# A hand-ordered weave of attention and MLP with three PSUM banks in turn and v scaled on Pool, on one Trainium2 core

## The chip, the cores and the metric

The kernel runs on one core of one Trainium2 chip. The metric is the device time of one execution in microseconds (us), median over the runs of a kernel. The profile covers the span from the first to the last instruction, which is 1 to 2.4 us shorter than the device time.

Names used below: PE is the tensor engine (PEld its weight loads), DVE the vector engine, ACT the scalar engine, POOL or Pool the GpSimd engine, SP the queue that issues most DMA. A *pair* is two heads of one batch element; there are 32 pairs, four per batch element.

## The reference

```python
# q, k, v: (8, 8, 576, 64)   omega: (128, 64)   w_in: (512, 2048)   w_out: (2048, 512)
def phi(x):                                     # x already scaled by 1/sqrt(sqrt(64))
    h = x @ omega.T - (x * x).sum(-1, keepdims=True) / 2
    return exp(h - h.max(-1, keepdims=True)) / sqrt(128)
kv  = einsum('bhsm,bhsd->bhmd', phi(k), v);  z = phi(k).sum(2)
att = einsum('bhsm,bhmd->bhsd', phi(q), kv) / (einsum('bhsm,bhm->bhs', phi(q), z) + 1e-6)
x   = att.transpose(0, 2, 1, 3).reshape(4608, 512)
h   = x @ w_in
out = (h * sigmoid(1.702 * h)) @ w_out          # float32
```

Both kernels use bf16 products. They drop what cancels in the ratio (the row factor of phi(q)), and divide v by the row maximum of exp(k-projection), which is the same as subtracting the maximum first.

## The kernel before

One head at a time is loaded, projected and normalised. A scheduler with priorities interleaves this with the MLP of finished tokens. Loads take 64 floats (256 bytes) per run, because a partition gets one token's head row.

```python
ps_tq = ...(bufs=2)   # transposes and q projection
ps_k  = ...(bufs=1)   # k projection, two banks
ps_nk = ...(bufs=1)
ps_h  = ...(bufs=2)   # first MLP product: two banks
ps_o  = ...(bufs=1)   # second MLP product: one bank
# ... (cut)
nc.gpsimd.dma_start(qkh[:, :, 0:64],
    qrows[row0 : row0 + SPAD, :].rearrange("(t p) d -> p t d", p=128))   # 256-byte runs, cast to bf16
# ... (cut)
def moe_block(tok0, ntok):                       # 512 tokens
    for f in range(NFC):                         # 16 quanta of the first product
        ph = ps_h.tile(...)
        for c in range(CM): nc.tensor.matmul(ph[:, 0:ntok], lhsT=win[...], rhs=xt[c][...], ...)
        nc.scalar.activation(out=th, in_=ph, func=AF.Tanh, scale=0.851)
        nc.vector.scalar_tensor_tensor(out=gT[:, f, 0:ntok], in0=th, scalar=1.0, in1=ph, op0=ALU.add, op1=ALU.mult)
    for r0 in range(0, ntok, 128):
        po = ps_o.tile(...)
        for f in range(NFC): nc.tensor.matmul(po[0:m, :], lhsT=gT[:, f, r0 : r0 + m], rhs=wout[:, f, :], ...)
        nc.scalar.activation(out=osb, in_=po, func=AF.Copy, scale=0.5)
        nc.sync.dma_start(out[...], osb)
```

The softmax here doesn't subtract the row's maximum and nothing guards it: scores larger than these inputs give would overflow.

Of the kernel before, what the change touches and what calls it, by code (L numbers as in the profile page):

```python
# [10 lines left out]
AF = mybir.ActivationFunctionType  # L12
ALU = mybir.AluOpType
# [3 lines left out]


@with_exitstack
def kernel(  # L20
# [10 lines left out]
    nc = tc.nc  # L31

    B, H, S, D = q.shape
    M_F = omega.shape[0]
    DM = H * D
    DFF = moe_w_in.shape[1]
    NT = B * S
    SCALE = 1.0 / math.sqrt(math.sqrt(D))

    assert M_F == 128 and D == 64 and DM == 512 and S == 576  # L40
    NCH = 5
    SPAD = NCH * 128
    CM = DM // 128
    NFC = DFF // 128
    TOK_BLK = 512
    last_b0 = (B - 1) * S
    blocks = []
    t0 = 0
    while t0 + TOK_BLK <= last_b0:
        blocks.append((t0, TOK_BLK))  # L50
        t0 += TOK_BLK
    if t0 < last_b0:
        blocks.append((t0, last_b0 - t0))
        t0 = last_b0
    while t0 < NT:
        n = min(TOK_BLK, NT - t0)
        blocks.append((t0, n))
        t0 += n

    const = ctx.enter_context(tc.tile_pool(name="const", bufs=1))  # L60
    xtp = ctx.enter_context(tc.tile_pool(name="xt", bufs=1))
    stage = ctx.enter_context(tc.tile_pool(name="stage", bufs=3))
    work = ctx.enter_context(tc.tile_pool(name="work", bufs=3))
    small = ctx.enter_context(tc.tile_pool(name="small", bufs=4))
    xbp = ctx.enter_context(tc.tile_pool(name="xb", bufs=2))
    gtp = ctx.enter_context(tc.tile_pool(name="gt", bufs=2))
    thp = ctx.enter_context(tc.tile_pool(name="th", bufs=3))
    osbp = ctx.enter_context(tc.tile_pool(name="osb", bufs=2))
    ps_tq = ctx.enter_context(tc.tile_pool(name="ps_tq", bufs=2, space=bass.MemoryType.PSUM))
    ps_k = ctx.enter_context(tc.tile_pool(name="ps_k", bufs=1, space=bass.MemoryType.PSUM))  # L70
    ps_nk = ctx.enter_context(tc.tile_pool(name="ps_nk", bufs=1, space=bass.MemoryType.PSUM))
    ps_h = ctx.enter_context(tc.tile_pool(name="ps_h", bufs=2, space=bass.MemoryType.PSUM))
    ps_o = ctx.enter_context(tc.tile_pool(name="ps_o", bufs=1, space=bass.MemoryType.PSUM))

    prio_stack = ExitStack()
    prio_stack.enter_context(tc.high_priority(offset=3_000_000))
    ident = const.tile([128, 128], BF16, name="ident")
    make_identity(nc, ident[:])

    om_f = const.tile([128, D], F32, name="om_f")  # L80
    nc.sync.dma_start(om_f[:], omega[:, :])
    om_b = const.tile([128, D], BF16, name="om_b")
    nc.vector.tensor_copy(out=om_b[:], in_=om_f[:])
    omT2 = const.tile([128, M_F], BF16, name="omT2")
    omt_ps = ps_tq.tile([128, SPAD], BF16, name="omt_ps", tag="tq")
    nc.tensor.transpose(omt_ps[0:64, 0:128], om_b[:], ident[:])
    nc.vector.tensor_copy(out=omT2[0:64, :], in_=omt_ps[0:64, 0:128])
    nc.vector.tensor_copy(out=omT2[64:128, :], in_=omt_ps[0:64, 0:128])

    win = const.tile([128, CM, DFF], BF16, name="win")  # L90
    wout = const.tile([128, NFC, DM], BF16, name="wout")

    win_pieces = [(c, j) for c in range(CM) for j in range(4)]
    wout_pieces = list(range(NFC))

    def load_win_piece(c, j):
        nc.gpsimd.dma_start(
            win[:, c, j * 512 : (j + 1) * 512],
            moe_w_in[c * 128 : (c + 1) * 128, j * 512 : (j + 1) * 512],
        )  # L100

    woutst = ctx.enter_context(tc.tile_pool(name="woutst", bufs=4))
    wout_stage = {}

    def load_wout_piece(f):
        t = woutst.tile([128, 1, DM], F32, name="wout_p", tag="wout_p")
        nc.sync.dma_start(t[:, 0, :], moe_w_out[f * 128 : (f + 1) * 128, :])
        wout_stage[f] = t

    def cast_wout_piece(f):  # L110
        nc.vector.tensor_copy(out=wout[:, f : f + 1, :], in_=wout_stage[f][:])

    xt = [xtp.tile([128, NT], BF16, name=f"xt{c}", tag=f"xt{c}") for c in range(CM)]
    prio_stack.close()

    qrows = q.rearrange("b h s d -> (b h s) d")
    krows = k.rearrange("b h s d -> (b h s) d")

    def attention_head(b: int, h: int, xb):
        qkh = stage.tile([128, NCH, 128], BF16, name="qkh", tag="qkh")  # L120
        vst = stage.tile([128, NCH, 65], F32, name="vst", tag="vst")
        row0 = (b * H + h) * S
        if (b, h) != (B - 1, H - 1):
            nc.gpsimd.dma_start(  # L124
                qkh[:, :, 0:64],
                qrows[row0 : row0 + SPAD, :].rearrange("(t p) d -> p t d", p=128),
            )
            nc.gpsimd.dma_start(  # L128
                qkh[:, :, 64:128],
                krows[row0 : row0 + SPAD, :].rearrange("(t p) d -> p t d", p=128),  # L130
            )
        else:
            nc.gpsimd.dma_start(
                qkh[:, 0:4, 0:64], q[b, h, 0:512, :].rearrange("(t p) d -> p t d", p=128)
            )
            nc.gpsimd.dma_start(
                qkh[:, 0:4, 64:128], k[b, h, 0:512, :].rearrange("(t p) d -> p t d", p=128)
            )
            nc.gpsimd.memset(qkh[64:128, 4, :], 0.0)
            nc.gpsimd.dma_start(qkh[0:64, 4, 0:64], q[b, h, 512:576, :])  # L140
            nc.gpsimd.dma_start(qkh[0:64, 4, 64:128], k[b, h, 512:576, :])
        nc.gpsimd.memset(vst[64:128, 4, :], 0.0)
        nc.gpsimd.memset(vst[:, 0:4, 64:65], 1.0)
        nc.gpsimd.memset(vst[0:64, 4, 64:65], 1.0)
        nc.sync.dma_start(
            vst[:, 0:4, 0:64], v[b, h, 0:512, :].rearrange("(t p) d -> p t d", p=128)
        )
        nc.sync.dma_start(vst[0:64, 4, 0:64], v[b, h, 512:576, :])

        qkTp = ps_tq.tile([128, SPAD], BF16, name="qkTp", tag="tq")  # L150
        for t in range(NCH):
            nc.tensor.transpose(qkTp[:, t * 128 : (t + 1) * 128], qkh[:, t, :], ident[:])  # L152
        qkT = work.tile([128, SPAD], BF16, name="qkT", tag="qkT")
        nc.vector.tensor_copy(out=qkT[:], in_=qkTp[:])  # L154

        qeT = work.tile([128, SPAD], BF16, name="qeT", tag="qeT")
        for c0, cn in ((0, 512), (512, 128)):
            pq = ps_tq.tile([128, 512], F32, name="pq", tag="tq")
            nc.tensor.matmul(pq[:, 0:cn], lhsT=omT2[0:64, :], rhs=qkT[0:64, c0 : c0 + cn])  # L159
            nc.scalar.activation(  # L160
                out=qeT[:, c0 : c0 + cn], in_=pq[:, 0:cn], func=AF.Exp, scale=SCALE
            )

        pk = ps_k.tile([128, NCH, 128], F32, name="pk", tag="pk")
        for t in range(NCH):
            nc.tensor.matmul(  # L166
                pk[:, t, :],
                lhsT=qkT[64:128, t * 128 : (t + 1) * 128],
                rhs=omT2[64:128, :],
            )  # L170
        ke = work.tile([128, NCH, 128], BF16, name="ke", tag="ke")
        nc.scalar.activation(out=ke[:], in_=pk[:], func=AF.Exp, scale=SCALE)  # L172
        maxE = small.tile([128, NCH], F32, name="maxE", tag="maxE")
        nc.vector.reduce_max(out=maxE[:], in_=ke[:], axis=AX.X)  # L174
        emax = small.tile([128, NCH], F32, name="emax", tag="emax")
        nc.vector.reciprocal(out=emax[:], in_=maxE[:])
        vp = work.tile([128, NCH, 65], BF16, name="vp", tag="vp")
        nc.vector.tensor_tensor(  # L178
            out=vp[:],
            in0=vst[:],  # L180
            in1=emax[:].unsqueeze(2).to_broadcast([128, NCH, 65]),
            op=ALU.mult,
        )

        nk = ps_nk.tile([128, 512], F32, name="nk", tag="nk")
        kvp = nk[:, 447:512]
        for t in range(NCH):
            nc.tensor.matmul(  # L188
                kvp,
                lhsT=ke[:, t, :],  # L190
                rhs=vp[:, t, :],
                start=(t == 0),
                stop=(t == NCH - 1),
            )
        kvs = work.tile([128, 65], BF16, name="kvs", tag="kvs")
        nc.scalar.activation(out=kvs[:], in_=kvp, func=AF.Copy)

        nd = nk[:, 0:NCH * 65].rearrange("p (t c) -> p t c", t=NCH)
        for t in range(NCH):
            nc.tensor.matmul(  # L200
                nd[:, t, :],
                lhsT=qeT[:, t * 128 : (t + 1) * 128],
                rhs=kvs[:],
            )
# [119 lines left out]
```

## Time and profile before

| | before |
|---|---|
| device time, median of 2 | 433.06 us (432.79 to 433.33) |
| span of the profile | 431.9 us |
| first MLP matmul starts | 53.29 us |
| last PE instruction ends | about 428.0 us |
| DMA packets under 512 bytes | 124,032 of 132,778 |

From the page of the kernel before: the busy tenths of PE in 40 equal slices of the span (a 9 is 90% or more), and the start of the chain that ended last, as shares of the span by line.

```profile
PE   0066597889988899989999899989999999999895
...
PE po L260 18%; PE ph L237 12%; DVE gT L248 3%; ACT th L245 3%; ACT osb L268 1%; ACT qeT L160 1%; PE qkTp L152 1%; PE nk L200 1%; PE xps L222 0%; PE pq L159 0%; PE nk L188 0%; DVE vp L178 0%; ACT ke L172 0%; DVE xb L209 0%; PE pk L166 0%
```

PE does almost nothing in the first two slices and is near full later. In the chain, lines 248, 245 and 268 (gT on DVE, th and osb on ACT) hold about 7%, 31 us, in which some later matmul waited for them.

From the chain in order of time, kernel before, in the stretch where only MLP work is left. The columns are start in us, length in us, and what ran (xN counts instructions).

```profile
311.44 0.93 PE ph L237 x4
...
312.40 0.61 ACT th L245
...
313.03 0.70 DVE gT L248
...
313.77 1.04 PE ph L237 x4
```

Four matmuls (0.87 us at full pace), then tanh, then gT, and only then the next four into that bank: this is the round of one of the two ph banks. PE's own timeline of the same stretch shows what it did meanwhile (start, length, line, operation and shape; xN counts instructions):

```profile
312.20 0.38 PE L237 MATMUL ph<-xt_116,win 128*128 128x512 bf16 x1
...
313.07 0.59 PE L260 MATMUL po<-wout,gT 128*128 128x512 bf16 x2
313.77 0.38 PE L237 MATMUL ph<-xt_116,win 128*128 128x512 bf16 x1
```

A block of 512 tokens takes 29.1 us here, where 128 matmuls at their 0.2157 us spacing would take 27.6.

From PE's timeline of the kernel before, in the woven part (start, length, line, operation and shape; xN counts instructions). The operation `ph` is the MLP, `pq` and `pk` are the q and k projections, 64 rows each.

```profile
219.31 0.38 PE L237 MATMUL ph<-xt_119,win 128*128 128x512 bf16 x1
219.63 0.38 PE L159 MATMUL pq<-qkT,omT_106 64*128 64x512 bf16 x1
219.64 0.40 PE L166 MATMUL pk<-omT_106,qkT 64*128 64x128 bf16 x4
219.85 0.22 PE L159 MATMUL pq<-qkT,omT_106 64*128 64x128 bf16 x1
219.87 0.22 PE L166 MATMUL pk<-omT_106,qkT 64*128 64x128 bf16 x1
220.02 0.39 PE L260 MATMUL po<-wout,gT 128*128 128x512 bf16 x1
```

pq and pk start together: they sit in different row halves of the array.

### The profile page before, as it was taken

The page shows a single profiled execution, that of the slowest core. Times are in us where ns is not written, and L with a number is a line of the kernel's source. Part 1 is how long each engine was busy: PE and PEld are TensorE (multiplying, and loading weights), DVE is VectorE, ACT ScalarE, POOL GpSimd, SP SyncE. Part 2 cuts the span into 40 slices and gives each one's busy share as a digit, 9 for nine tenths or more (in the row PEclk, how much of TensorE's full clock was granted, in tenths as well). Part 3 has the DMA queues.
Part 4 walks back from the last instruction along what each step waited for, and adds up shares of the span by engine and source line. Part 5 has one row for each costly group of instructions (what it writes and reads, how often), then busy time and mean ns, then how long its engine had stood idle before and what let it go on. Part 6 is the DMA issues. An engine that isn't in the chain of part 4 may idle for free. (4 is left out here: it accounts for less than half of the span.)

```text
span 431.9 us, 8223 instructions
## 1 busy us (share of the span) xinstructions
PE 372.1 (86%) x2801; PEld 189.3 (44%) x2801; DVE 276.9 (64%) x787; ACT 208.5 (48%) x454; POOL 139.3 (32%) x345
## 2 busy tenths in 40 slices
PE   0066597889988899989999899989999999999895
PEld 0044344454555454445455445444434444444342
DVE  1378769897799878889789878872351441523501
ACT  1044166565576545666467546633452433434412
POOL 8378256256266157256356336000000000000000
PEclk9999999999999999999999999999999999999999
DMA  9999589579799479669879759101101001011011
GB/s 163 248 257 174 63 67 103 66 73 139 120 80 97 70 85 143 93 54 124 130 79 101 81 74 133 38 2 49 50 0 73 27 24 74 1 49 38 7 67 37
DMA packets 132778, 36.21 MB, mean 84 GB/s; under 512 B 124032, under 2 KB 126080, under 8 KB 132736
## 3 DMA queue, kind: packets, MB, share of 16 engines
q0 software_dynamic: 86176, 12.58, 41.5%
q1 hardware_dynamic: 46560, 23.11, 19.4%
q8 instruction: 22, 0.36, 0.4%
q14 instruction: 20, 0.16, 0.1%
HBM read 38.80 MB, written 9.44 MB: 112 GB/s over the span
## 5 line engine op out<-in xcount | busy, mean ns | idle before, releaser
L260 PE MATMUL po<-wout,gT 128*128 128x512 bf16 (+1 forms) x592 | 163.5, 380 | 3.3 <-ACT osb L268 1.8
L248 DVE SCALAR_TENSOR_TENSOR gT<-th,ph 128x512 bf16<-128x512 bf16 (+2 forms) x160 | 99.2, 625 | 93.5 <-ACT th L245 92.8
L245 ACT ACTIVATE th<-ph 128x512 bf16<-128x512 f32 (+2 forms) x160 | 88.4, 555 | 69.1 <-PE ph L237 57.5
L237 PEld LDWEIGHTS <-win 128*128 128x128 bf16 x640 | 56.2, 98 | 58.2 <-issue 13.3
L124 POOL DMA_DIRECT2D qkh<-in_q_dram x63 | 54.7, 868 | 82.0 <-PE qkTp L152 69.6
L260 PEld LDWEIGHTS <-gT 128*128 128x128 bf16 (+1 forms) x592 | 53.7, 98 | 55.2 <-DVE gT L248 5.8
L160 ACT ACTIVATE qeT<-pq 128x512 bf16<-128x512 f32 (+1 forms) x128 | 49.2, 435 | 56.8 <-PE pq L159 43.9
L237 PE MATMUL ph<-xt_116,win 128*128 128x512 bf16 (+2 forms) x160 | 57.2, 360 | 8.4 <-DVE gT L248 6.6
L174 DVE TENSOR_REDUCE maxE<-ke 128x5 f32<-128x640 bf16 x64 | 52.1, 814 | 8.3 <-ACT ke L172 8.1
L237 PE MATMUL ph<-xt_117,win 128*128 128x512 bf16 (+2 forms) x160 | 57.3, 361 | 0.0
L237 PE MATMUL ph<-xt_118,win 128*128 128x512 bf16 (+2 forms) x160 | 57.0, 359 | 0.0
L237 PE MATMUL ph<-xt_119,win 128*128 128x512 bf16 (+2 forms) x160 | 57.0, 359 | 0.0
L128 POOL DMA_DIRECT2D qkh<-in_k_dram x63 | 54.8, 871 | 1.8 <-DMA qkh<-in_k_dram 0.8
L268 ACT ACTIVATE osb<-po 128x512 f32<-128x512 f32 (+1 forms) x37 | 22.1, 598 | 67.6 <-PE po L260 67.6
L159 PE MATMUL pq<-qkT,omT_106 64*128 64x512 bf16 (+1 forms) x128 | 31.8, 320 | 17.5 <-DVE qkT L154 17.3
L172 ACT ACTIVATE ke<-pk 128x640 bf16<-128x640 f32 x64 | 45.6, 712 | 0.3
L152 PE MATMUL qkTp<-ident,qkh 128*128 128x128 bf16 x320 | 31.2, 230 | 12.3 <-DMA qkh<-in_k_dram 5.9
L154 DVE COPY qkT<-qkTp 128x640 bf16<-128x640 bf16 x64 | 30.9, 483 | 12.7 <-PE qkTp L152 11.3
L152 PEld LDWEIGHTS <-qkh 128*128 128x128 bf16 x320 | 24.3, 102 | 33.0 <-issue 28.4
L178 DVE TENSOR_TENSOR vp<-vst,emax 128x325 bf16<-128x325 f32 x64 | 30.6, 478 | 1.4 <-DVE rden L208 0.4
L209 DVE TENSOR_TENSOR xb<-nk,rden 128x320 bf16<-128x320 f32 x64 | 31.0, 484 | 0.3
L166 PE MATMUL pk<-omT_106,qkT 64*128 64x128 bf16 x320 | 31.1, 230 | 0.0
(38 smaller groups left out, 263.1 us busy)
## 6 DMA issues: line engine op xcount, KB each, us to landing
out_dram<-osb SPq DMA_DIRECT2D x35, 256.0 KB, 2.0
vst<-in_v_dram SPq DMA_DIRECT2D x64, 128.0 KB, 2.7
qkh<-in_q_dram POOLq DMA_DIRECT2D x63, 80.0 KB, 3.1
qkh<-in_k_dram POOLq DMA_DIRECT2D x63, 80.0 KB, 3.4
wout_p<-in_moe_w_out_dram SPq DMA_DIRECT2D x16, 256.0 KB, 6.1
win<-in_moe_w_in_dram POOLq DMA_DIRECT2D x16, 128.0 KB, 6.6
vst<-in_v_dram SPq DMA_DIRECT2D x64, 16.0 KB, 2.7
out_dram<-osb SPq DMA_DIRECT2D x2, 128.0 KB, 2.3
```

The costliest lines, as they stand in the source:

```text
L124: nc.gpsimd.dma_start(qkh[:, :, 0:64], qrows[row0 : row0 + SPAD, :].rearrange("(t p) d -> p t d", p=128),)
L128: nc.gpsimd.dma_start(qkh[:, :, 64:128], krows[row0 : row0 + SPAD, :].rearrange("(t p) d -> p t d", p=128),)
L152: nc.tensor.transpose(qkTp[:, t * 128 : (t + 1) * 128], qkh[:, t, :], ident[:])
L159: nc.tensor.matmul(pq[:, 0:cn], lhsT=omT2[0:64, :], rhs=qkT[0:64, c0 : c0 + cn])
L160: nc.scalar.activation(out=qeT[:, c0 : c0 + cn], in_=pq[:, 0:cn], func=AF.Exp, scale=SCALE)
L166: nc.tensor.matmul(pk[:, t, :], lhsT=qkT[64:128, t * 128 : (t + 1) * 128], rhs=omT2[64:128, :],)
L172: nc.scalar.activation(out=ke[:], in_=pk[:], func=AF.Exp, scale=SCALE)
L174: nc.vector.reduce_max(out=maxE[:], in_=ke[:], axis=AX.X)
L237: nc.tensor.matmul(ph[:, 0:ntok], lhsT=win[:, c, f * 128 : (f + 1) * 128], rhs=xt[c][:, tok0 : tok0 + ntok], start=(c == 0), stop=(c == CM ...
L245: nc.scalar.activation(out=th[:, 0:ntok], in_=ph[:, 0:ntok], func=AF.Tanh, scale=0.851)
L248: nc.vector.scalar_tensor_tensor(out=gT[:, f, 0:ntok], in0=th[:, 0:ntok], scalar=1.0, in1=ph[:, 0:ntok], op0=ALU.add, op1=ALU.mult,)
L260: nc.tensor.matmul(po[0:m, :], lhsT=gT[:, f, r0 : r0 + m], rhs=wout[:, f, :], start=(f == 0), stop=(f == NFC - 1),)
```

## The change

Its intent: q, k and v come in pairs of heads, with 9 tokens of 64 floats per partition, so 2304-byte runs; both heads of a pair use the two row halves of the array; batch 0 is ordered by hand; from then on the MLP is cut into 288 *quanta* of four 512-column matmuls, and every step of a pair has a fixed quantum. The three MLP banks are separate tiles used in turn by both products. In batch 0 v is scaled on Pool. The diff, cut to its core:

```diff
-    ps_h = ctx.enter_context(tc.tile_pool(name="ps_h", bufs=2, space=bass.MemoryType.PSUM))
-    ps_o = ctx.enter_context(tc.tile_pool(name="ps_o", bufs=1, space=bass.MemoryType.PSUM))
+        tr = psum.tile([128, 1024], BF16, name="tr")          # transposes, one bank
+        pqk = psum.tile([128, 2, 512], F32, name="pqk")       # projections
+        nd = psum.tile([128, 2, 512], F32, name="nd")         # kv, numerator, denominator, rest of K
+        mo = [psum2.tile([128, 512], F32, name=f"mo{i}") for i in range(3)]
+    def pairs_of(x):
+        return x.rearrange("b (c e) (p t) d -> (b c) (e p) (t d)", e=2, t=NS)
+        def load_v(i, eng=nc.sync):
+            eng.dma_start(t[:], vv[i])
+        def KV(i):                                            # head e in row half e
+            for s in range(NS):
+                for e in range(2):
+                    nc.tensor.matmul(nd[:, e, 0:65], lhsT=ke[64 * e : 64 * e + 64, s, :],
+                                     rhs=t[64 * e : 64 * e + 64, s, :], ...)
+        def X(i, tr=tr):
+            for g in range(NG):
+                n = 128 if g < 4 else 64
+                nc.tensor.transpose(tr[:, g * 128 : g * 128 + n], xb[0:n, g, :], ident[0:n, 0:n])
... (cut: batch 0 by hand)
+        A(2)                   # transposes and their evictions
+        C(1)                   # q projection
+        Dv(1)                  # hm, m, em, and v scaled on Pool
+        load_win(2)
+        Bk(2)                  # K projection and its exps
+        ND(0)
+        xm(0)
+        expQ(1, pq2[:])
+        KV(1)
+        kvs(1)
+        A(3)
... (cut: the weave; s is the first quantum of pair i)
+                at(s, lambda: T1(i), lambda: evT1(i))
+                at(s + 1, lambda: T2(i), lambda: evT2(i))
+                at(s + 2, lambda: K(i))
+                at(s + 2, lambda: KV(i - 1), lambda: kvs(i - 1))
+                at(s + 2, lambda: expM(i), lambda: expK(i))
+                at(s + 3, lambda: ND(i - 1))
+                at(s + 3, lambda: mx0(i))                     # hm
+                at(s + 4, lambda: xm(i - 1))                  # xb
+                at(s + 5, lambda: Q(i, pqk), lambda: mx1(i), lambda: expQ(i, pqk[:]))
+                at(s + 6, lambda: X(i - 1), lambda: evX(i - 1))
+                at(s + 6, lambda: vp(i))
+                dst = mo[nb % 3][:]
```

Pairs 4 to 8 start every 5 quanta, from quantum 5, the later ones every 8.

## The prediction

> **What bounds the kernel now.** Three stretches, read from PE's timeline. (1) Start: the first MLP matmul begins at 53.3 us; until then PE waits on loads and on batch 0's chain through PE, ACT and DVE. (2) Weave, 53 to about 288 us: PE is 89 to 94% busy in the windows table, partly small matmuls and modelled tails. (3) Pure MLP, 288 to 432 us: five blocks, 29.1 us each in the chain of waits. A 512-column matmul starts every 0.2157 us, so a block of 128 needs 27.6 us, all nine 248.4 us. The chain gives DVE gT 3.1%, ACT th 2.7%, ACT osb 1.4%: 31 us in which PE stands because the two ph banks and the one po bank aren't free.
>
> **What the change does, costed from the trace.**
> - Start. q, k, v arrive as pairs of heads in 2304-byte runs instead of 256-byte ones. From packet times (a 2 KB run cast on the POOL queue takes about 0.1 us on one of 16 engines) a pair needs about 2.6 us, batch 0 about 10 us; before, 256-byte runs (32 ns each) competed with wout, and the first qkT copy came at 19.5 us. Four pairs at about 3.7 us (ACT: two exps of 1024 at 0.95 us; evictions) plus about 10 us of chain: first MLP matmul at about 30 us (26 to 36). v scaled on Pool: 576 elements, 1.3 us, an estimate from the Trainium skill, "GPSIMD Engine Reference", section "Performance versus the Vector engine" (about 2.6 cycles per element for two inputs); the trace has no such Pool arithmetic. Gain about 23 us.
> - Three banks in turn. Matmuls 0.86, tanh 0.60, gT 0.70: about 2.25 us per round, over three banks 0.75, under PE's 0.86. MLP becomes PE bound, 27.6 us a block. Gain about 30 us, most of the chain's DVE and ACT share.
> - Attention on PE. Transposes space at 56 ns, 65-column matmuls at 32 ns; pq and pk already start together, on different row halves. With both heads' K, Q and kv products paired over row halves I estimate 2.2 to 2.3 us a pair against about 2.9 now. 28 woven pairs: gain about 17 us.
> - DVE per woven pair, from back-to-back spacing (duration less 0.08 us): 0.60 + 0.37 + 0.67 + 0.67 + 0.74 + 0.37 + two reciprocals 0.4 = 3.8 us. In eight first-product quanta with a pair: DVE 4.9 + 3.8 = 8.7 us, ACT about 7.3, PE 6.9 + 2.2 = 9.1. PE leads only narrowly, so I add about 11 us of stalls, including the first pairs (every five quanta), where transposes wait for evictions of the one tr tile and qk tiles 5 to 7 land behind wout.
>
> **Sum.** 30 + 248.4 + 28 x 2.25 (63) + 11 stalls + 3 tail = about 355 us.
>
> Predicted: 355 us, 338 to 374 in 8 of 10. Faster by over 2%: 0.97; within: 0.02; slower: 0.01.
>
> **What would show it.** First MLP matmul near 30 us; last two blocks 27.6 us each, PE starts 0.216 us apart, no gT or th in the chain; blocks with four pairs 37 to 39 us; DVE about 90% busy in first-product stretches; DMA packets under 512 B nearly gone; Pool vp near 1.3 us.
>
> **What would make it wrong.** Pool vp at 2 us or more, setting the start's cadence, since DMA issue shares its queue; pair loads no faster; PE idle long in the start and then at half rate (0.43 us spacing at 53 us before); a fixed order stalling PE on every DVE or ACT delay (up to 375 us); paired row halves not overlapping for the kv product (plus 0.3 us a pair, 8 us).

## The result, and the profile after

| | before | after |
|---|---|---|
| device time, median of 2 | 433.06 us | 377.36 us (377.04 to 377.68) |
| span of the profile | 431.9 us | 375.9 us |
| first MLP matmul starts | 53.29 us | 35.58 us |
| first MLP matmul to the last | 374.7 us | 335.6 us |
| an unwoven MLP block | 29.1 us | 27.7 us |
| DMA packets under 512 bytes | 124,032 | 2,960 |

The ratio is 0.8703 (95% interval 0.8653 to 0.8753): the mean time of one kernel's fast runs over that of the other's of the same rounds, so not quite the ratio of the medians quoted. The change is a clear gain, but 377.4 us lies above the predicted range of 338 to 374. Of the 56.0 us that the span lost, 17.7 came from the start and 39.1 from the time between the first and the last MLP matmul; the tail grew by 0.8.

What the 39.1 us are made of can be read from both traces, by adding up the times from the start of one MLP matmul to the start of the next:

| between MLP matmuls, us | before | after |
|---|---|---|
| their own spacing at full rate | 252.1 | 248.5 |
| beyond it, where attention work lies between | 106.5 | 81.5 |
| beyond it, where nothing lies between | 15.9 | 5.5 |

Attention on PE, with the waits inside it, gave back 25 us, where the prediction had put 17. The MLP's own standing gave back 10.4, of 15.9 that there were to give, where the prediction had put 30 (waits for MLP banks that fall into the second row can't be told apart). The first row fell by 3.6 us because the kernel before cuts the tokens into eight blocks of 512, one of 448 and one of 64, and so needs 592 matmuls of the second product, where nine blocks need 576.

From the page of the changed kernel, the two lines that answer to those of before:

```profile
PE   6557998899999999999999999999999999999995
...
PE mo L301 30%; PE mo L281 17%; DVE gT L295 10%; ACT th L291 4%; DVE xb L255 4%; DVE m L201 3%; DVE qkT L118 2%; DVE vp L214 2%; PE nd L243 2%; PE nd L225 2%; ACT ke L172 2%; PE tr L266 2%; DVE xt L272 2%; DMA qk<-in_q_dram 2%; PE tr L108 2
```

The share of gT and th in the chain is still 14%. This is no contradiction, as the next views show: it all lies in the woven part. The chain at the end of the changed kernel:

```profile
315.86 13.92 PE mo L281 x64
329.77 13.81 PE mo L301 x64
343.59 13.81 PE mo L281 x64
357.40 13.83 PE mo L301 x64
```

In the last two blocks PE is the whole chain: 64 matmuls in 13.8 us, 0.216 us each. That is what three banks were meant to do. In the woven part the chain runs differently; here is one stretch of the first product (the 16 first quanta of a block):

```profile
126.96 0.64 ACT th L291
...
127.62 0.69 DVE gT L295
...
128.47 0.82 DVE xb L255
129.30 0.60 DVE gT L295
129.89 0.68 DVE m L201
...
130.72 0.63 DVE gT L295
131.35 0.37 DVE xt L272
131.72 0.67 DVE vp L214
132.38 1.20 DVE gT L295 x2
133.58 0.61 DVE qkT L118
...
134.23 0.22 PE tr L143
```

The lines left out here are small (reciprocals, and `issue` pieces of at most 0.09 us). From 127.6 to 134.2 us DVE works without a pause worth the name, and PE (`tr` at 134.23) waits for its end. Two windows of eight quanta each with one pair, the first in the first product and the second in the second product. The columns are length, busy time (and count) of PE, PEld, DVE, ACT and POOL, then granted clock (of PE, as the profile records it; 1.00 is full speed), DMA share and GB/s:

```profile
122.98:133.45 10.47, 10.06 (x89) 4.93 (x87) 8.92 (x17) 7.61 (x16) 1.05 (x2) 1.00 0.50 124
144.31:153.78 9.47, 9.47 (x87) 4.81 (x86) 4.11 (x8) 4.10 (x9) 1.05 (x2) 1.00 0.49 97
```

Eight quanta alone need 8 x 0.863 = 6.90 us. In the second product they took 9.47, with DVE only 4.1 us busy, so a pair costs PE 2.57 us. In the first product they took 10.47: 1.0 us more, with DVE 8.9 us busy. Only one of the two pairs in a first product stalls like this; the rest of it (19.9 - 10.5) takes 9.4. As a check on 2.57: the six places where a pair breaks into the MLP in the trace, where nothing is waited for, cost PE 0.45 (eight transposes), 0.14 (the ninth), 0.77 (K and kv), 0.31 (numerator and denominator), 0.42 (Q) and 0.45 us (output transposes), 2.53 in all.

The sum that was predicted, term by term, on the span. The pairs' 72.0 is 28 x 2.57, and the stalls are what is left of 335.6:

| term | predicted | measured |
|---|---|---|
| start, to the first MLP matmul | 30 | 35.6 |
| nine blocks of MLP matmuls | 248.4 | 248.4 (0.2157 us each) |
| 28 woven pairs on PE | 63 | 72.0 |
| stalls | 11 | 15.2 |
| tail | 3 | 4.7 |
| outside the span | 0 | 1.5 |
| sum | 355 | 377.4 |

The largest error is the cost of a pair on PE, 9.0 us, then the start, 5.6 us.

### The profile page after: what moved, and what is told of

It reads as the page before. It is cut to its first block, busy times and chain, and to the rows that moved or that the text cites. A ratio compares the mean times of both kernels' runs of the same rounds, so it can differ in the third digit from the quotient of the medians.

```text
span 375.9 us, 7120 instructions
## 1 busy us (share of the span) xinstructions
PE 347.6 (92%) x2888; PEld 174.1 (46%) x2888; DVE 219.7 (58%) x408; ACT 199.3 (53%) x401; POOL 48.1 (13%) x90
## 2 busy tenths in 40 slices
DMA packets 23728, 32.99 MB, mean 88 GB/s; under 512 B 2960, under 2 KB 15248, under 8 KB 23696
## 4 chain that ended last, share of the span: by engine, by line
PE 60%; DVE 24%; ACT 8%; issue 4%; DMA 2%; POOL 1%; ACTq 0%; DVEq 0%; POOLq 0%
PE mo L301 30%; PE mo L281 17%; DVE gT L295 10%; ACT th L291 4%; DVE xb L255 4%; DVE m L201 3%; DVE qkT L118 2%; DVE vp L214 2%; PE nd L243 2%; PE nd L225 2%; ACT ke L172 2%; PE tr L266 2%; DVE xt L272 2%; DMA qk<-in_q_dram 2%; PE tr L108 2%
## 5 line engine op out<-in xcount | busy, mean ns | idle before, releaser
L281 PE MATMUL mo<-xt,win 128*128 128x512 bf16 x576 | 140.1, 382 | 2.6 <-DVE gT L295 2.6
L301 PE MATMUL mo<-wout,gT 128*128 128x512 bf16 x576 | 139.3, 382 | 0.0
L295 DVE SCALAR_TENSOR_TENSOR gT<-th,mo 128x512 bf16<-128x512 bf16 x144 | 96.9, 679 | 34.9 <-ACT th L291 34.4
L291 ACT ACTIVATE th<-mo 128x512 bf16<-128x512 f32 x144 | 86.4, 601 | 47.9 <-PE mo L281 46.1
L301 PEld LDWEIGHTS <-gT 128*128 128x128 bf16 x576 | 51.1, 98 | 59.3 <-issue 9.7
L311 ACT ACTIVATE osb<-mo 128x512 f32<-128x512 f32 x36 | 21.5, 598 | 37.5 <-PE mo L301 32.2
L191 ACT ACTIVATE qe<-pqk 128x1024 bf16<-128x1024 f32 x28 | 28.6, 1021 | 23.3 <-PE pqk L182 23.3
L172 ACT ACTIVATE ke<-pqk 128x1024 bf16<-128x1024 f32 x32 | 33.3, 1040 | 0.9 <-PE pqk L153 0.7
L255 DVE TENSOR_TENSOR xb<-nd,r 128x640 bf16<-128x640 f32 x32 | 26.4, 824 | 1.1
L201 DVE TENSOR_REDUCE m<-hm 128x9 f32<-128x576 bf16 x32 | 23.9, 747 | 0.1
L118 DVE COPY qkT<-tr 128x1024 bf16<-128x1024 bf16 x28 | 19.1, 682 | 6.0 <-PE tr L108 6.0
```

The lines of the kernel that those rows point to most:

```text
L118: nc.vector.tensor_copy(out=st[i]["qkT"][:, 0:8, :], in_=src[:])
L172: nc.scalar.activation(out=st[i]["ke"][:, 1:9, :].rearrange("p (j e) f -> p e j f", e=2), in_=pqk[:].rearrange("p e (j f) -> p e j f", f=128),
L191: nc.scalar.activation(out=dst, in_=s, func=AF.Exp, scale=SCALE)
L201: nc.vector.reduce_max(out=m[:], in_=st[i]["hm"][:], axis=AX.X)
L255: nc.vector.tensor_tensor(out=xb[:].rearrange("p g e d -> p e g d"), in0=v4[:, :, :, 0:64], in1=r[:].unsqueeze(3).to_broadcast([128, 2, NG ...
L281: nc.tensor.matmul(dst, lhsT=win[:, c, f * 128 : (f + 1) * 128], rhs=xt[c][:, n * 512 : (n + 1) * 512], start=(c == 0), stop=(c == NC_ - 1),)
```

## The experiments

Each is an edit of the changed kernel (377.4 us, ratio 0.870) unless it says otherwise, timed in 3 rounds against the kernel before, and all gave correct results. The changed kernel itself was timed only twice (377.04 and 377.68 us), the experiments four times each, so a difference of less than about 1 us in the total isn't clear of the noise. "A woven block" means the blocks in the middle, with four pairs: 39.25 us in the changed kernel, 19.9 in the first product and 19.3 in the second, counted from the timeline of PE between the changes of product.

### Two banks instead of three (e1_two_banks)

```diff
-                dst = mo[nb % 3][:]
+                dst = mo[nb % 2][:]
```

> One edit: the MLP products use two of the three separate banks in turn. If a bank is busy for matmul 0.86 + tanh 0.60 + gT 0.70 us with hand-overs (about 2.25), two banks allow one first-product quantum per 1.12 us instead of 0.86: +4 us in each of the two unwoven first-product stretches and +4 to +8 us in each of the seven woven ones, so 415 to 440 us, most of the change's gain gone. Rival: the third bank matters little, because the second product is bound by the tensor engine and the vector engine sets the woven first-product stretches anyway: below 390 us.

Measured: 409.3 us, ratio 0.945 (0.943 to 0.946). The first product of a woven block rose from 19.9 to 23.5 us, that of an unwoven block from 13.8 to 19.4. Here is the chain in an unwoven block of this run:

```profile
369.49 0.88 PE mo L281 x4
...
370.39 0.61 ACT th L291
...
371.02 0.70 DVE gT L295
...
371.76 1.04 PE mo L281 x4
```

It is the pattern of the kernel before. The rival (below 390) falls, and so does the size of the theory: 32 us, not 38 to 63. The unwoven first products lost 5.6 us each, more than the 4 expected, but the woven ones 3.5 and not 4 to 8, and the first block only 1.9 in all. (That stalls which were there already now hide behind these is likely, but not shown.) So in this kernel, with its fixed order, 32 us hang on the third bank. That is not its share of the gain over the kernel before: that one also had only two ph banks, but its scheduler ran the second product in between, so its MLP stood for 15.9 us in all (table above).

### v of batch 0 on DVE (e2_v_on_dve)

```diff
-            vp(i, pool=True)
+            vp(i)
```

> v of batch 0 scaled on the vector and scalar engines as in the weave, not on Pool. Pool takes 1.14 us and a hand-over, the vector engine 0.75, but it is also needed for the copies and maxima of the neighbouring pairs. If Pool's slower arithmetic sits on the start's chain, the MLP begins up to 1.5 us earlier; if the relief of the vector engine is worth it, up to 2 us later. Total 375 to 379 us either way.

Measured: 379.4 us, ratio 0.875; the MLP began at 37.3 us instead of 35.6. Pool's scaling takes 1.14 us against DVE's 0.75, and still shortens the start by about 1.8 us, since DVE has copies and maxima of the next pair to do.

### hm one quantum later (e3_hm_late)

```diff
-            if new:
-                at(s + 3, lambda: mx0(i))
             if old:
                 at(s + 4, lambda: xm(i - 1))
+            if new:
+                at(s + 4, lambda: mx0(i))
```

> One edit of order: the elementwise max hm of a woven pair is issued one quantum later on the vector engine, behind the normalisation xb. Head-of-line theory: in woven first-product stretches the vector engine stands about 0.9 us at hm waiting for the exp of ke, with gT queued behind it, and pays back by stalling the tensor engine about 1 us per pair; then eight such quanta shrink from 10.46 us to 9.5 to 10 and the time falls by 5 to 13 us (364 to 372). Throughput theory (the vector engine simply has too much work there): no change, 376 to 379.

Measured: 384.0 us, ratio 0.885, slower. The first product of a woven block went to 20.5 us. The head-of-line theory fell, and plain throughput over the whole stretch doesn't predict a loss either. DVE's timeline in this run shows why:

```profile
130.16 0.69 DVE L295 SCALAR_TENSOR_TENSOR gT<-th,mo 128x512 bf16<-128x512 bf16 x1 [1.36 <-ACT th L291]
...
131.01 0.82 DVE L255 TENSOR_TENSOR xb<-nd,r 128x640 bf16<-128x640 f32 x1
131.75 0.45 DVE L197 TENSOR_TENSOR hm<-ke 128x576 bf16<-128x576 bf16 x1
```

The hole stays. With hm gone DVE waits 1.36 us for th instead, and hm now adds to the run of work behind the hole. So in this order hm had used time that nothing else could use.

### The exp of ke one quantum later (e9_exp_late)

After that run the suspect was ACT: in the changed kernel, kvs, two small exps and the exp of ke stand in front of a tanh.

```diff
-                at(s + 2, lambda: expM(i), lambda: expK(i))
+                at(s + 2, lambda: expM(i))
-                at(s + 3, lambda: mx0(i))
+                at(s + 3, lambda: expK(i))
+                at(s + 4, lambda: mx0(i))          # behind xm(i - 1)
```

> Order only, on the changed kernel: the exp of ke (1.04 us) of a woven pair is issued one quantum later on the scalar engine, behind the tanh of that quantum, and hm one quantum later behind xb. Second theory of the woven stalls: not hm but the scalar engine's block of kvs, two small exps and the exp of ke (1.9 us) holds back a tanh, so gT comes late and in a burst; then the first-product stretch falls from 19.9 to 19.2 us or less, 3 to 5 us in all (372 to 374). If the stalls come from the amount of work on the vector engine after that point, no gain or a loss as in the run with hm late (377 to 384).

Measured: 375.4 us, ratio 0.866. A woven block's first product went from 19.9 to 19.8, its second from 19.3 to 19.2. The second theory falls in its size as well: 0.2 us a block where 0.7 was expected. The rest of the 2 us came in the first block, and isn't shown to come from the edit: a stretch at half rate in that block, which costs 1.55 us in the changed kernel's trace (see below), is missing in this one.

### v scaled on Pool throughout (e4_pool_weave)

```diff
-                at(s + 6, lambda: vp(i))
+                at(s + 6, lambda: vp(i, pool=True))
```

> The v scaling of every woven pair goes to Pool as in batch 0 (1.14 us there), taking 0.67 us off the vector engine and 0.24 us off the scalar engine per pair. Throughput theory: woven first-product stretches give back 0.67 us per pair, 14 pairs, about 9 us (368 us); second-product stretches don't change. Head-of-line theory: the burst behind hm gets shorter by 0.67 us too, so 4 to 9 us; if Pool gets in the way of the vector engine or delays the kv product, no gain or a loss.

Measured: 373.4 us, ratio 0.8615 (0.859 to 0.864), 4 us less where the throughput theory had 9. A woven block is 38.4 us, 0.5 less in the first product and 0.4 in the second. Four pairs at 2.57 and 27.6 of MLP make 37.9, so stalls were 1.35 us a woven block and about 0.5 are left. The most that this edit could win in the weave was thus about 8 us, not 9, and most of a block's stalls are now gone. The traces say what PE waited for. In a woven block of the changed kernel it waits for gT at 131.40 us (the matmul starts 0.63 us after the one before instead of 0.22) and at 133.03, and for the copy of qkT out of the one `tr` tile at 134.23 and, in the second product, at 144.09 (0.69 instead of 0.22). With v on Pool one wait for gT is left in such a block (130.56 us, 0.70 instead of 0.22), and this is the 0.5. What the three runs show together: taking work out of DVE's unbroken run of 6.6 us shortens the stalls; moving work around it won 0.2 us a block (e9) or lost 0.7 (e3). That this run is the cause of every stall is not shown.

### The last transpose over all 128 rows (e5_x_full)

```diff
-                n = 128 if g < 4 else 64
-                nc.tensor.transpose(tr[:, g * 128 : g * 128 + n], xb[0:n, g, :], ident[0:n, 0:n])
+                nc.tensor.transpose(tr[:, g * 128 : (g + 1) * 128], xb[:, g, :], ident[:])
```

> The last of the five output transposes of a pair takes all 128 rows instead of 64 (the upper rows hold finite filler and are not evacuated). Theory: the 64-row transpose changes the array's row mode and back; the stretch from the first transpose to the next MLP matmul is now 0.45 us where four 128-column transposes and a short one should take 0.26 to 0.28; it falls to about 0.28 to 0.30, 28 pairs, 4 to 5 us (372 to 373 us). Rival: that time has another cause; no change.

Measured: 374.5 us, ratio 0.864 (0.863 to 0.865). PE's timeline of this run, and after it that of the changed kernel. `pqk<-qkT` at line 182 is Q; lines 265 and 266 are the output transposes (X):

```profile
147.11 0.39 PE L182 MATMUL pqk<-qkT,omT 64*128 64x512 bf16 x2
147.43 1.04 PE L300 MATMUL mo<-wout,gT 128*128 128x512 bf16 x4
148.30 0.44 PE L265 MATMUL tr<-ident,xb 128*128 128x128 bf16 x5
148.58 1.67 PE L300 MATMUL mo<-wout,gT 128*128 128x512 bf16 x7
```

```profile
148.78 0.39 PE L182 MATMUL pqk<-qkT,omT 64*128 64x512 bf16 x2
149.11 1.04 PE L301 MATMUL mo<-wout,gT 128*128 128x512 bf16 x4
149.98 0.52 PE L266 MATMUL tr<-ident,xb 128*128 128x128 bf16 x5
150.43 1.90 PE L301 MATMUL mo<-wout,gT 128*128 128x512 bf16 x8
```

From the first transpose to the next MLP matmul it is 0.28 us instead of 0.45, for more columns: the 64-row transpose had cost 0.17 us of changing over. The mode theory holds, and the gain is 2.8 us and not 4.8: a woven block fell by only 0.3 us where four pairs should save 0.7. Where PE soon waits for DVE anyway, part of the saving is given back: its wait for gT in such a block grew from 0.26 to 0.43 us, that for qkT in the second product from 0.31 to 0.40.

### Q over all 128 rows (e12_q_full)

```diff
-                    lhsT=omT[64 * e : 64 * e + 64, :],
-                    rhs=t[64 * e : 64 * e + 64, 4:8, :].rearrange("p j c -> p (j c)"),
+                    lhsT=omZ[:, e, :],             # omega of head e, zeros in the other half's rows
+                    rhs=t[:, 4:8, :].rearrange("p j c -> p (j c)"),
```

> On the changed kernel, the two Q products of a pair take all 128 rows, with omega padded by zeros in the other head's rows, so they no longer run side by side but don't change the array's row mode either. Now the Q slot costs 0.42 us: 0.22 of matmuls and gaps of 0.09 before and 0.11 after it. Mode-change theory: the gaps vanish and the matmuls take 0.43, so the slot stays at 0.43 us and the time at 376 to 379 us. If the gaps have another cause they remain: 0.63 us a slot, 28 slots, 382 to 384 us.

Measured: 377.7 us, ratio 0.873. The slot of Q in this run:

```profile
147.11 1.89 PE L302 MATMUL mo<-wout,gT 128*128 128x512 bf16 x8
148.84 0.59 PE L183 MATMUL pqk<-qkT,omZ 128*128 128x512 bf16 x2
149.27 1.03 PE L302 MATMUL mo<-wout,gT 128*128 128x512 bf16 x4
```

Eight MLP matmuls from 147.11 end at 148.84, and Q starts at once; two matmuls of 0.216 later the MLP goes on, with no gap. In the changed kernel (above) two paired Q matmuls take 0.33 us from start to next start, and 0.09 us of standing before them. So the gaps belong to the change of row mode, and for Q running both heads side by side saves 0.22 us and pays 0.20 for it: nothing is won. The Trainium skill, "TensorEngine Tiling (Array Packing)", section "Key Properties", says that changing the tiling mode drains the tensor engine; traces agree, and put 0.09 to 0.11 us on each change.

### K and kv products in head order (e6_unpaired)

```diff
-            for j in range(4):
-                for e in range(2):
+            for e in range(2):
+                for j in range(4):
...
-            for s in range(NS):
-                for e in range(2):
+            for e in range(2):
+                for s in range(NS):
```

> K and kv products of a pair in head order (all of the first head, then all of the second) instead of alternating row halves. If the alternation makes the two halves overlap, K should grow from about 0.28 to 0.5 us and kv from 0.38 to 0.65, 0.5 us per pair, about 14 us in all (385 to 392 us). Rival: the products do not overlap much as they are, or overlap in either order: 376 to 380 us.

Measured: 383.6 us, ratio 0.885, half of what the pairing theory expected. kv grew from 0.38 to 0.56 us, so its halves do overlap when they alternate. K stayed at 0.29 us in either order; why, no run here tells. A woven block grew by 0.7 us, four times what kv grew by.

### v of pairs 4 to 7 later (e7_late_v)

```diff
-        load_v(4)
+        load_v(4, nc.gpsimd)
...
-            load_v(i)
+            load_v(i, nc.gpsimd)
```

> The v loads of pairs 4 to 7, which the sync queue issues at 1.2 us ahead of everything (1.2 MB against the first pairs' q and k), are issued from Pool in program order instead. If the start is bound by loads, the first qkT copy moves from 7.8 to about 5.8 us, the MLP begins 2 to 3 us earlier than 35.6 and the time falls by the same (374 to 375 us). If it is bound by the chain of engines from pair 1 on, the copy comes earlier but the MLP begins at most 1.5 us earlier (376 us or more).

Measured: 376.65 us, ratio 0.868. The first qkT copy came at 5.59 us instead of 7.80, and the MLP began at 33.83 instead of 35.58; the total fell by only 0.7 us. Program order on the SP queue had sent four loads of later pairs at 1.2 us, because nothing held them back. They did cost the first pair 2 us. The MLP's gain of 1.75 us lies between the two expectations (2 to 3, at most 1.5). The qkT copies of the later pairs came 4.75 and 6.13 us apart, as in the changed kernel, so after the first pairs it is not these loads that set the pace.

### Another order of batch 0 (e8_start_order)

What the start waits on, from the timeline of all engines of the changed kernel, from pair 2's exps to pair 1's kv, in two cuts (start and length in us, then engine, line and work; in brackets at the end, the idle time before and what ended it):

```profile
17.94 1.14 POOL L214 TENSOR_TENSOR vp<-v,em 128x576 bf16<-128x576 f32 x1
18.07 0.27 ACT L163 ACTIVATE ke<-nd 128x128 bf16<-128x128 f32 x1
18.23 0.28 ACT L164 ACTIVATE qe<-nd 128x128 bf16<-128x128 f32 x1
...
18.56 0.71 PE L243 MATMUL nd<-kvs,qe 128*128 128x65 bf16 x10 [1.35 <-ACT qe L164]
```

```profile
19.38 0.22 DVE L252 RECIPROCAL r<-nd 128x10 f32<-128x10 f32 x1 [1.68 <-PE nd L243]
19.64 0.82 DVE L255 TENSOR_TENSOR xb<-nd,r 128x640 bf16<-128x640 f32 x1
...
20.52 0.68 PE L225 MATMUL nd<-vp,ke 64*128 64x65 bf16 x18 [1.25 <-DVE xb L255]
```

ND of pair 0 (`nd<-kvs,qe`, line 243) waits 1.35 us, until the small exps of pair 2 have read their part of `nd`; kv of pair 1 (line 225) waits 1.25 us, until xb of pair 0 has read it. One tile, three uses, in the order of the program: a pair takes 6.1 us (qkT copies at 15.75 and 21.88). Pool's 1.14 us of v for pair 1 ended at 19.1 us, 1.4 us before kv of pair 1 could start, so it was not what that product waited for.

```diff
+        A(2)
         KV(0)
         kvs(0)
-        A(2)
-        C(1)
         Dv(1)
         load_win(2)
-        Bk(2)
         ND(0)
         xm(0)
+        C(1)
+        Bk(2)
         expQ(1, pq2[:])
+        A(3)
         KV(1)
         kvs(1)
-        A(3)
... (cut: the same for the later pairs)
```

> Only the hand order of batch 0 changes: the numerator and denominator matmuls and xb of pair i are issued before the K product of pair i+2, and the transposes of the next pair before the kv product. Chain theory: from pair 1 to 3 the start goes at 6.1 us a pair because these steps queue behind each other through the one nd tile; with the new order about 4 us a pair, the MLP begins at 31 to 33 us instead of 35.6, total 373 to 375. Load theory: no change (the MLP begins at 35 to 36).

Measured: 372.4 us, ratio 0.859 (0.858 to 0.860), and the MLP began at 31.05 us instead of 35.58. The chain theory holds; the load theory falls. In the changed kernel's start PE waits 4.4 us in all to begin a kv product because xb has not yet read `nd`; in this run's trace that wait is gone. The edit moves the transposes too, so what the `nd` order alone is worth wasn't tested.

### The parts together (e10_combined)

The edits of e8, e7, e5 and e4, and `expM` ahead of `expK` in batch 0.

> The parts that helped alone, together: new start order (minus 5.0 us alone), small exps ahead of the exp of ke in the start, v of pairs 4 to 7 late (minus 0.7), full last transpose (minus 2.8), v scaled on Pool throughout (minus 4.0). If they add: 364 to 366 us, MLP beginning at 28.5 to 30.5 us, a woven block 38.0 us instead of 39.25. If the transpose and Pool savings sit on the same stalls they overlap: 366 to 369.

Measured: 365.0 us, ratio 0.842 (0.840 to 0.843); the MLP began at 29.4 us, and a woven block took 38.0. The gains alone (5.0, 0.7, 2.8, 4.0) add up to 12.5, and the sum shows 12.4. So close a fit is partly luck: `expM` ahead of `expK` was never run alone, and the 0.7 isn't clear of the noise.

### Fillers in the start (e11_filled)

```diff
+        def fill(n, dst):
+            for _ in range(n):
+                nc.tensor.matmul(dst, lhsT=zero[:, 0:128], rhs=zero[:])
         def Bk(i):
+            fill(3, pqk[:, 0, :])
             K(i)
...
+        fill(8, mo[2][:])
         X(3, tr)
```

> The combined kernel with idle-time matmuls on zeros in the start (three ahead of each K product, eight ahead of the last output transpose). If low activity keeps the tensor engine at half rate until about 39 us, and the fillers raise it, the first 24 MLP matmuls take 5.2 us instead of 6.6 and the chain's matmuls shrink: 1.5 to 4 us less than the combined kernel. If the half rate stays, the fillers cost up to 1.5 us.

Measured: 366.8 us, ratio 0.846: slower than e10. The fillers did what they should: 24 MLP matmuls went by in 5.2 us, against 7.9 in e10. But they put the MLP's start off to 31.1 us, and PE then stood 2.0 us at the transposes of pair 5 for its k, which was loaded behind the second MLP weight. One wait had hidden the other.

### Loads of pairs 5 and 6 ahead of the second weight (e13_qk_first, e14_qk_first_filled)

```diff
+        for i in range(5, 7):
+            load_qk(i)
+            load_v(i, nc.gpsimd)
         for j in range(4):
             load_wout(j)
-        for i in range(5, 8):
+        for i in range(7, 8):
```

e13 is e10 with this edit, e14 is e11 with it.

> The combined kernel with q, k and v of pairs 5 and 6 loaded ahead of the second MLP weight. There the tensor engine waited only 0.3 us for such a load, so if the half rate holds the first block nothing changes (364.5 to 365.5 us); if the loads do, 1 us less. If the second MLP weight then comes too late for quantum 16, up to 3 us more.

> The same with the fillers on zeros. In the filled kernel the wait of 2.0 us for a load stood where the half rate had been. If that is all, moving the loads ahead gives back 2 us of 366.8 (364.5 to 365), and against the run without fillers the full rate is worth at most 1 us, as the fillers themselves delay the MLP's beginning by up to 1.7 us. If the second MLP weight now comes too late, it is above 366.

Measured: e13 363.55 us (361.7 to 365.2), ratio 0.837 (0.835 to 0.840); e14 363.0 us (362.3 to 364.2), ratio 0.838 (0.836 to 0.840). The waits for these loads are gone from both. With fillers the gain was 3.7 us, more than the 2.0 that stood there; without, 1.5. The two don't differ clearly from each other, so full rate in the start bought nothing that shows beyond the noise once the loads were moved. These are the fastest versions here; both beat the kernel before and the changed one.

## Why the prediction was wrong

- **The step that failed most: "I estimate 2.2 to 2.3 us a pair against about 2.9 now."** Measured: 2.57 us, 9.0 of the 22 us. The estimate named no cost for the changes between 128-row and 64-row work. In the changed kernel a pair goes into 64-row work and back for Q (0.09 and 0.11 us), for K with kv (0.10 and 0.09) and for the last transpose (0.17 together), some 0.55 us; without them a pair would take about 2.0, so the rest was put a little high. The run with Q over 128 rows shows it for Q, that with the full transpose for X; for K with kv it is read from the trace alone. The prediction read from the trace that pq and pk start together, and overlooked the 0.10 us on each side of them. The kernel before spent 106.5 us for 28 pairs in gaps with attention work, 3.8 each with the waits in them; so the gain over it was larger than predicted, although the new cost was underestimated.
- **"Four pairs at about 3.7 us ... first MLP matmul at about 30 us": 35.6.** The 3.7 us were ACT's work per pair. The hand order made it 6.1 us between pairs 2 and 3, a chain through the one nd tile. Order alone gave back 4.5 us of start (e8), the v loads sent early 1.8 (e7, alone). Loads and Pool were not the limit after pair 1, although Pool vp (1.14 us, estimated 1.3 from the skill's page) was right, and worth about 1.8 us.
- **Stalls, 11 predicted: 15.2.** The woven blocks stalled 1.35 us each; the first block took 45.8 us instead of 27.6 + 5 x 2.57 = 40.5. Of these 5.3 us, 1.3 are a PE at half rate after the idle start (24 matmuls in 6.5 us instead of 5.2), and 1.55 a second such stretch from 58.6 to 62.2 us, after PE had waited 1.1 and 0.5 us for DVE (matmuls up to 0.43 us apart, granted clock 0.58 from 58 to 62 us). The other 2.5 are waits in the dense pairs, by subtraction. The second stretch is also in the traces of e2, e3, e6, e7 and e13 (second product of the first block 25.8 to 26.6 us), and missing in the other nine (23.7 to 24.7), so two single traces can differ by 1.5 us there. For the first stretch the spacing is the witness, not the granted clock: from 35.6 to 38 us it is recorded as 1.00 in the changed kernel and 0.50 in e4, with the same 0.43 us between matmuls.
- **"PE leads only narrowly": right in the mean.** DVE was 85% busy in woven first-product quanta, and PE stalled there all the same, where the work comes in a run of 6.6 us.
- **Three banks: "27.6 us a block" was right**, 27.7 measured, no gT or th in the chain there. **"31 us in which PE stands", and with it "gain about 30 us", was wrong**: it took shares of the chain for idle time of PE. The MLP stood for 15.9 us before and 5.5 after. The total didn't suffer, since the sum was built from the new kernel's costs alone. That e1 lost 32 us is another quantity, and its nearness to 30 is luck.
- **Small packets nearly gone: right.** Blocks with four pairs were put at 37 to 39 us and took 39.25.

Left open: why K doesn't care about the order of its halves, and why the second stretch at half rate comes in some runs and not in others.

## What to carry to other kernels

Cost small matmuls with the gaps around them, not by their columns: find one in the trace and measure from the end of the work before to the start of the work after. When an order is fixed by hand, follow one shared tile through all of its writers and readers and count the round trip, since the mean load of each engine says nothing about it. Before a share of the chain is booked as a gain, look at the engine's own timeline: it may have had other work. A load that nothing holds back goes out at once, in front of those that are needed first.

## What the Trainium skill lacked or had wrong

- "TensorEngine Tiling (Array Packing)", Key Properties: it says that a mode change drains but gives no size. Here each change costs 0.09 to 0.11 us, so that two 64-row matmuls of 512 columns side by side (0.42 us with gaps) are no faster than two of 128 rows in turn (0.43).
- "TensorE: Matmul & The Clock Gate", the part on the transpose: nothing warns that a transpose of 64 rows counts as such a change. Here one among four full ones cost 0.17 us.
- "GPSIMD Engine Reference", Performance versus the Vector engine: its 2.6 cycles per element gave an estimate of 1.25 us for 576 elements; measured, with one operand broadcast, 1.14 us, a tenth less.
- No page weighs matmuls on zeros as a filler for an idle start: here they brought 24 matmuls from 7.9 to 5.2 us, and nothing clear in the total.
